# Talking-heads attention with a squared-ReLU FFN: turning q and k straight from their loaded layout, scores a block earlier, deeper gathers

## Chip, cores, metric

The kernel runs on 1 core of one Trainium2 chip. The metric is device microseconds of one execution, as a median of runs. Engines: PE (matmul; PEld are its weight loads), DVE (vector), ACT (scalar), GpSimd (POOL in the profile), SP (issues DMAs). The few timed executions of the kernel before that were slow (one on chip 0, two on chip 7) are left out of the ratios.

## The reference

```python
# q, k, v: (8, 12, 448, 64); w_pre, w_post: (12, 12)
scores = np.matmul(q, k.transpose(0, 1, 3, 2)) / sqrt(64)
scores = np.einsum('bhij,hg->bgij', scores, w_pre)       # mix the heads
attn   = softmax(scores, axis=-1)
attn   = np.einsum('bhij,hg->bgij', attn, w_post)        # mix again
x      = np.matmul(attn, v)                              # -> (3584, 768)
h      = np.maximum(x @ w_in, 0)                         # w_in (768, 2048)
out    = (h * h) @ w_out                                 # w_out (2048, 768)
```

## The kernel before

Each batch of 448 query rows is cut into blocks of 120, 120, 120 and 88 rows, and each block into tiles of 10 rows by 12 heads, so that mixing the heads is one matmul. A *step* handles two tiles; a batch has 23 steps. The FFN of a batch is filler for PE during the next batch. In the code, `at_step(i, f)` runs `f` at step i, and `hurry(units, w)` queues units of work for PE that become due w filler slots later (four slots per step). Names in the profile: `raw` is q or k as loaded, `rows` the same in another order, `s_ps` and `sq` scores, `sx` a gathered tile, `m_ps` the first mixing, `e` its exp, `d` the normalised tile, `at_ps` and `at` the second mixing, `ot_ps` and `xt` the product with v, `h_ps`, `hr`, `h` and `o_ps` the FFN.

```python
    def to_rows(raw, key, eng, parts=1):          # L87: a reordering copy
        t = work.tile([PR, NR, H, D], BF16, name="rows", tag="rows", bufs=2)
        w = H // parts
        for y in range(parts):
            eng.tensor_copy(out=t[:, :, w*y:w*y+w, :].rearrange("p r h d -> p h r d"),
                            in_=raw[:, w*y:w*y+w, :, :])
        rows[key] = t
    # ... start: to_rows(kraw, ..., nc.vector, 2); to_rows(qraw, ..., nc.vector, 2) ...

    def turn_unit(key, c):                        # 8 transposes of 128 columns
        src = rows[key]
        # ...
        for y in range(2):
            for r in range(NR):
                p = 2 * c + y
                nc.tensor.transpose(ps[:, S*y + PR*r : S*y + PR*r + PR],
                    src[:, r, 2*p:2*p+2, :].rearrange("p h d -> p (h d)"), ident[0:PR, 0:PR])
        nc.vector.tensor_copy(out=dst[...], in_=ps[...])          # kt or qt

    def scores(b, t, c):                          # a third of a block's scores
        for p in (2 * c, 2 * c + 1):
            ps = pair_bank("s_ps")                # one of 3 PSUM pairs
            # ... two matmuls ...
            nc.scalar.copy(out=sq[:, 2*p:2*p+2, :], in_=ps[:, :, 0:S])

    def pre(s):                                   # m_ps matmuls into a PSUM pair, exp on ACT, then
            nc.vector.tensor_scalar(out=d[0:TR, 0:S], in0=e[0:TR, :], ...)        # L304
    def post(s, y):                               # at_ps matmuls into a PSUM pair, then
            nc.vector.tensor_copy(out=ats[...], in_=ps[...])      # L325 frees the pair

    # plan: k of the next batch is copied at step 6, q at step 12
    at_step(i0 + 6 + 6*n, lambda key=key: to_rows(raws.pop(key), key, nc.gpsimd))
    at_step(i0 + 6 + 6*n, lambda key=key: hurry(turn_units(key), 6))
    # main loop, per step: pre; fill; scores of the NEXT block at its steps 0, 1, 3;
    #   gathers up to AHEAD = 6 tiles; filler; post of two steps ago
```

The softmax here doesn't subtract the row's maximum and nothing guards it: scores larger than these inputs give would overflow.

## Time and profile before

| kernel before | value | where |
|---|---|---|
| time | 755.97 us, median of 2 (755.44 to 756.49) | timed runs |
| span of the profiled execution (it took 748.7 us, about 7 less than the timed ones) | 746.8 us | page |
| PE, DVE, ACT, GpSimd busy | 83, 66, 61, 30% | page |
| PE and PEld both idle, up to PE's last instruction | 120.8 us | worked out: their records laid together |
| batches 1 to 6 | 85.1 us each | worked out: from first `e` to first `e` |

The page of the kernel before: busy us, then the span in 40 slices, in tenths (PEclk is the granted clock).

```profile
span 746.8 us, 15596 instructions
PE 620.1 (83%) x5898; PEld 368.1 (49%) x5898; DVE 491.2 (66%) x868; ACT 451.9 (61%) x1097; POOL 226.6 (30%) x250
PE   3375679779978898889988898799989797899897
PEclk9986768999989999999999999999999999999999
...
L87 POOL COPY rows<-raw 112x3072 bf16<-112x3072 bf16 x14 | 40.7, 2904 | 22.3 <-DMA raw<-in_q_dram 15.9
L304 DVE TENSOR_SCALAR d_109<-e,rc 120x448 bf16<-120x448 f32 x60 | 48.7, 812 | 1.1
```

PE is the busiest engine. The clock dips in the first quarter, where PE has little work. The last two lines give busy us and mean ns of one. The mean of `d_109` is 812 ns while most instances take about 450 ns, so a few must be very long.

PE's waits between 60 and 650 us in the list of waits (us in total, times, longest):

```profile
PE s_ps L273 <- DVE at_120 L325: 17.2, 9, 3.9
PE m_ps L294 <- DMA sx<-sq: 15.8, 15, 3.6
PE s_ps L273 <- DVE at_119 L325: 8.4, 6, 2.8
PE s_ps L273 <- DVE at_118 L325: 8.2, 7, 2.3
...
```

Scores wait 34 us here for a PSUM pair that DVE's eviction of `at_ps` frees, and the first mixing waits 16 us for a gathered tile. Why DVE is late stands in the timeline around 216 us (start, us, engine, line, out<-in, count). First GpSimd:

```profile
216.02 2.74 POOL L87 COPY rows<-raw 112x3072 bf16<-112x3072 bf16 x1
218.72 0.93 POOL L218 TENSOR_TENSOR h_2795<-hr 128x448 bf16<-128x448 f32 x1
```

Then DVE in the same stretch:

```profile
216.35 3.55 DVE L304 TENSOR_SCALAR d_106<-e,rc 120x448 bf16<-120x448 f32 x1
219.82 1.13 DVE L304 TENSOR_SCALAR d_107<-e,rc 120x448 bf16<-120x448 f32 x1
220.87 1.15 DVE L325 CAST at_120<-at_ps 112x960 bf16<-112x960 f32 x1
```

And PE:

```profile
219.36 0.36 PE L273 MATMUL s_ps<-kt_71,qt_69 64*128 64x448 bf16 x2
222.07 0.37 PE L273 MATMUL s_ps<-kt_71,qt_69 64*128 64x448 bf16 x2 [2.35 <-DVE at_120 L325]
```

Read the three together. `d_106` starts just after the GpSimd copy has started and ends at 219.9, after the copy and the GpSimd instruction behind it. It took 3.55 us in place of 0.45. Of DVE's frequent instructions only those into `d` are stretched like this: the six evictions of `at_ps` that start during one of the copies of this run take 1.14 to 1.16 us, as elsewhere. The eviction behind it in DVE's order ends at 222.0, and the second half of the scores stands waiting for that pair for 2.35 us.

Whole view of the `d` line: the windows view for that line alone (stretch, its length, DVE busy with count, clock, DMA share, GB/s; the stretch is longer than any span, so it holds all).

```profile
0.00:820.00 820.00, 206.75 (x360) 0.95 0.51 90
```

360 instructions of 0.45 us, whose records overlap at their ends by some 15 us in all, would be about 148 us.

### The profile page before, as it was taken

To read this page: it belongs to the slowest core of one execution; us is meant where nothing else is said; L and a number is where in the kernel's file an instruction comes from. 1 tells how busy PE (TensorE), PEld (TensorE's weight loads), DVE (VectorE), ACT (ScalarE), POOL (GpSimd) and SP (SyncE) were. 2 spreads that over 40 slices of the span, in tenths; PEclk is the share of its full clock that TensorE was granted. 3 is DMA by queue.
4 is the path that set the end of the run, shared out by engine and by line. 5 is a ranking of instruction groups with operands and counts; after the bars stand their busy time and mean duration, and the time that the engine had idled before them with its cause. 6 is when DMAs were issued, how large, how long until landed. Compare 5 with 4: busy or idle time off the path is not lost. (4 is left out here: it accounts for less than half of the span.)

```text
span 746.8 us, 15596 instructions
## 1 busy us (share of the span) xinstructions
PE 620.1 (83%) x5898; PEld 368.1 (49%) x5898; DVE 491.2 (66%) x868; ACT 451.9 (61%) x1097; POOL 226.6 (30%) x250
## 2 busy tenths in 40 slices
PE   3375679779978898889988898799989797899897
PEld 2043445445545554455555554455545564455554
DVE  2166768786678766886678766787677766566400
ACT  2363577557666566676676566576676576685241
POOL 5351004561044400462044400562034400340070
PEclk9986768999989999999999999999999999999999
DMA  9869534885455565657446464637456455333202
GB/s 125 133 115 213 105 74 86 150 141 112 95 100 83 70 127 108 97 83 125 88 98 98 71 128 100 107 64 112 110 102 96 61 100 105 74 70 64 64 5 71
DMA packets 94735, 73.38 MB, mean 98 GB/s; under 512 B 7108, under 2 KB 94660, under 8 KB 94660
## 3 DMA queue, kind: packets, MB, share of 16 engines
q1 hardware_dynamic: 55682, 49.57, 32.0%
q0 software_dynamic: 38848, 22.81, 23.2%
q8 instruction: 46, 0.75, 0.4%
q14 instruction: 29, 0.24, 0.1%
q10 hardware_dynamic: 130, 0.01, 0.0%
HBM read 45.63 MB, written 11.01 MB: 76 GB/s over the span
## 5 line engine op out<-in xcount | busy, mean ns | idle before, releaser
L297 ACT ACTIVATE e<-m_ps 120x448 f32<-120x448 f32 x360 | 193.0, 544 | 134.5 <-issue 61.8
L275 ACT CAST sq<-s_ps 128x896 bf16<-128x896 f32 x192 | 166.6, 915 | 24.4 <-PE s_ps L273 24.4
L294 PE MATMUL m_ps<-sx,pre_w 120*128 120x448 bf16 x360 | 112.6, 385 | 37.1 <-DMA sx<-sq 32.5
L300 DVE RECIPROCAL rc<-sm 120x2 f32<-120x2 f32 (+1 forms) x184 | 29.9, 162 | 144.1 <-ACT e L297 143.8
L217 ACT ACTIVATE hr<-h_ps 128x448 f32<-128x448 f32 x128 | 70.3, 550 | 73.5 <-PE h_ps L213 56.6
L325 DVE CAST at_119<-at_ps 112x960 bf16<-112x960 f32 (+1 forms) x63 | 71.0, 1128 | 12.2 <-PE at_ps L320 11.5
L325 DVE CAST at_118<-at_ps 112x960 bf16<-112x960 f32 (+1 forms) x63 | 71.0, 1128 | 10.3 <-PE at_ps L320 9.7
L297 ACT ACTIVATION_READ_ACCUMULATOR e<-m_ps 120x1 f32 x360 | 73.5, 204 | 0.0
L325 DVE CAST at_120<-at_ps 112x960 bf16<-112x960 f32 (+1 forms) x58 | 65.8, 1135 | 7.3 <-PE at_ps L320 6.7
L248 ACT COPY osb<-o_ps 128x384 f32<-128x384 f32 x56 | 26.9, 480 | 56.2 <-PE o_ps L243 54.7
L273 PE MATMUL s_ps<-kt_71,qt_69 64*128 64x448 bf16 x192 | 34.4, 406 | 22.6 <-DVE at_120 L325 7.0
L273 PE MATMUL s_ps<-kt_72,qt_70 64*128 64x448 bf16 x192 | 32.2, 375 | 23.5 <-DVE at_120 L325 10.2
L294 PEld LDWEIGHTS <-pre_w 120*128 120x128 bf16 x360 | 32.5, 105 | 37.1 <-DMA sx<-sq 17.0
L304 DVE TENSOR_SCALAR d_109<-e,rc 120x448 bf16<-120x448 f32 x60 | 48.7, 812 | 1.1
L87 POOL COPY rows<-raw 112x3072 bf16<-112x3072 bf16 x14 | 40.7, 2904 | 22.3 <-DMA raw<-in_q_dram 15.9
L304 DVE TENSOR_SCALAR d_106<-e,rc 120x448 bf16<-120x448 f32 x60 | 46.2, 770 | 0.9
L213 PE MATMUL h_ps<-xt,w_0_126 128*128 128x448 bf16 x192 | 42.8, 363 | 0.1
L213 PE MATMUL h_ps<-xt,w_3_129 128*128 128x448 bf16 x192 | 41.2, 353 | 1.0 <-DVE xt L206 0.9
L165 PE MATMUL t_ps<-ident,rows 112*128 112x112 bf16 x384 | 35.4, 254 | 7.6 <-DVE rows L87 7.6
L213 PE MATMUL h_ps<-xt,w_1_127 128*128 128x448 bf16 x192 | 41.2, 353 | 0.2
L213 PE MATMUL h_ps<-xt,w_2_128 128*128 128x448 bf16 x192 | 41.1, 352 | 0.0
L206 DVE TENSOR_TENSOR xt<-ot_ps,bvec 128x360 bf16<-128x360 f32 (+1 forms) x64 | 31.7, 505 | 10.7 <-PE ot_ps L199 9.6
(475 smaller groups left out, 1200.9 us busy)
## 6 DMA issues: line engine op xcount, KB each, us to landing
sx<-sq SPq DMA_DIRECT2D x352, 105.0 KB
raw<-in_k_dram POOLq DMA_DIRECT2D x21, 224.0 KB, 7.6
raw<-in_q_dram POOLq DMA_DIRECT2D x21, 224.0 KB, 6.9
v_67<-in_v_dram POOLq DMA_DIRECT2D x12, 224.0 KB, 6.3
v_68<-in_v_dram POOLq DMA_DIRECT2D x12, 224.0 KB, 6.7
out_dram<-osb SPq DMA_DIRECT2D x16, 168.0 KB
out_dram<-osb SPq DMA_DIRECT2D x16, 144.0 KB
out_dram<-osb SPq DMA_DIRECT2D x16, 120.0 KB
```

The source lines that it names most:

```text
L87: eng.tensor_copy(out=t[:, :, w * y:w * y + w, :].rearrange("p r h d -> p h r d"), in_=raw[:, w * y:w * y + w, :, :])
L165: nc.tensor.transpose(ps[:, S * y + PR * r:S * y + PR * r + PR], src[:, r, 2 * p:2 * p + 2, :].rearrange("p h d -> p (h d)"), ident[0:PR, ...
L206: nc.vector.tensor_tensor(out=xts[b][:, cs, BQ * t:BQ * t + n], in0=pv[:, :, 0:n], in1=bvecs[b][:, cs].unsqueeze(2).to_broadcast([P, 3, n] ...
L213: nc.tensor.matmul(ps[:, 0:S], lhsT=w1[ft // 4][:, c2, 128 * (ft % 4):128 * (ft % 4) + 128], rhs=xts[b][:, c2, :], start=(c2 == 0), stop=( ...
L217: nc.scalar.activation(out=hr[:, :], in_=ps[:, 0:S], func=ACT.Relu)
L273: nc.tensor.matmul(ps[:, hh, 0:S], lhsT=qt[x][r, p, BQ * t:BQ * t + 128], rhs=kt[x][r, p, :], start=True, stop=True)
L275: nc.scalar.copy(out=sq[:, 2 * p:2 * p + 2, :], in_=ps[:, :, 0:S])
L294: nc.tensor.matmul(ps[:, y, 0:S], lhsT=pre_w[0:rows, :], rhs=sx[0:rows, :], start=True, stop=True)
L297: nc.scalar.activation(out=e[0:TR, :], in_=ps[0:TR, y, 0:S], func=ACT.Exp, scale=SCALE, accum_out=sm[0:TR, y:y + 1])
L300: nc.vector.reciprocal(out=rc[0:TR, 0:len(ms)], in_=sm[0:TR, 0:len(ms)])
L304: nc.vector.tensor_scalar(out=d[0:TR, 0:S], in0=e[0:TR, :], scalar1=rc[0:TR, y:y + 1], scalar2=1.0 / S, op0=ALU.mult, op1=ALU.subtract)
L325: nc.vector.tensor_copy(out=ats[(b, t)][0:PR, :, :, i0:i0 + TQ * n].rearrange("p r g (y i) -> p y (r g) i", i=TQ), in_=ps[0:PR, 0:n, 0:NR ...
```

## The change

Intent: (A) drop the reordering copies and transpose each head from the loaded layout, into the lower or upper 64 partitions, and give `raw` a second buffer; the transposes also become due one filler slot after their step, in place of six; (B) issue a block's scores about a block earlier; (C) gather up to ten tiles ahead in place of six; also a third `hr` buffer.

```diff
-    rows = {}
-    def to_rows(raw, key, eng, parts=1): ...
-    kraw, qraw = new_raw(), vt[1]
+    kraw, qraw = new_raw(), new_raw()          # raw: bufs 1 -> 2
-    to_rows(kraw, ("k", 0), nc.vector, 2)
-    to_rows(qraw, ("q", 0), nc.vector, 2)
...
-                p = 2 * c + y
-                nc.tensor.transpose(ps[:, S * y + PR * r:S * y + PR * r + PR],
-                                    src[:, r, 2 * p:2 * p + 2, :].rearrange("p h d -> p (h d)"), ident[0:PR, 0:PR])
+                for hh in range(2):
+                    nc.tensor.transpose(ps[64 * hh:64 * hh + 64, S * y + PR * r:S * y + PR * r + PR],
+                                        src[:, 4 * c + 2 * y + hh, r, :], ident[0:PR, 0:PR])
...                                             # hr: bufs 2 -> 3, sx: bufs 7 -> 12
-    AHEAD = 6
+    AHEAD = 10
-                at_step(i0 + 6 + 6 * n, lambda key=key: to_rows(raws.pop(key), key, nc.gpsimd))
-                at_step(i0 + 6 + 6 * n, lambda key=key: hurry(turn_units(key), 6))
+                at_step(i0 + 6 + 6 * n, lambda key=key: hurry(turn_units(key), 1))
+    for n in range(1, len(blocks)):            # first[x]: first step of block x
+        for c in range(3):
+            bursts.setdefault(first[blocks[n - 1]] - 1 + c, []).append((n, c))
...                                             # main loop
-                at_steps = (0, 1, 2) if t == 3 else (0, 1, 3)
-                if nb < len(blocks) and j in at_steps:
-                    scores(*blocks[nb], at_steps.index(j))
...
+                for n, c in bursts.get(i, []):
+                    scores(*blocks[n], c)
...
```

More of the change, by code (lines that the diff above doesn't have):

```diff
@@ L73, in new_raw @@
     def new_raw():
-        return work.tile([PR, H, NR, D], BF16, name="raw", tag="raw", bufs=1)
+        return work.tile([PR, H, NR, D], BF16, name="raw", tag="raw", bufs=2)
     def load_heads(t, src, b, h0, n):
@@ L78, in load_heads @@
                             in_=src[b, h0:h0 + n].rearrange("h (p r) d -> p h r d", r=NR))
-    rows = {}
-    def to_rows(raw, key, eng, parts=1):
-        t = work.tile([PR, NR, H, D], BF16, name="rows", tag="rows", bufs=2)
-        w = H // parts
-        for y in range(parts):
-            eng.tensor_copy(out=t[:, :, w * y:w * y + w, :].rearrange("p r h d -> p h r d"),
-                            in_=raw[:, w * y:w * y + w, :, :])
-        rows[key] = t
-    kraw, qraw = new_raw(), vt[1]
+    kraw, qraw = new_raw(), new_raw()
+    raws = {("k", 0): kraw, ("q", 0): qraw}
     for h0 in (0, 6):
@@ L157, in turn_unit @@
     def turn_unit(key, c):
-        src = rows[key]
+        src = raws[key]
         dst = (kt if key[0] == "k" else qt)[key[1] % 2]
@@ L215, in ffn1_unit @@
         h2 = work.tile([P, S], BF16, name="h2", tag="h2", bufs=FT + 1)
-        hr = work.tile([P, S], F32, name="hr", tag="hr", bufs=2)
+        hr = work.tile([P, S], F32, name="hr", tag="hr", bufs=3)
         nc.scalar.activation(out=hr[:, :], in_=ps[:, 0:S], func=ACT.Relu)
@@ L279, in gather @@
         n = min(TQ, BLOCKS[t] - TQ * m)
-        sx = work.tile([P, S], BF16, name="sx", tag="sx", bufs=7)
+        sx = work.tile([P, S], BF16, name="sx", tag="sx", bufs=12)
         nc.sync.dma_start(out=sx[0:H * n, :], in_=sqs[(b, t)][TQ * m:TQ * m + n, :, :])
@@ L367 @@
     until = [0]
-    raws = {}
     def start_raw(key):
@@ L388 @@
                         raws[key], src, b + 1, 4 * y, 4))
-                at_step(i0 + 6 + 6 * n, lambda key=key: to_rows(raws.pop(key), key, nc.gpsimd))
-                at_step(i0 + 6 + 6 * n, lambda key=key: hurry(turn_units(key), 6))
+                at_step(i0 + 6 + 6 * n, lambda key=key: hurry(turn_units(key), 1))
             for y in range(3):
                 at_step(i0 + 13 + y, lambda y=y, b=b: load_heads(vt[(b + 1) % 2], v, b + 1, 4 * y, 4))
+    first = {}
+    for i, (b, t, ms) in enumerate(steps):
+        first.setdefault((b, t), i)
+    bursts = {}
+    for n in range(1, len(blocks)):
+        for c in range(3):
+            bursts.setdefault(first[blocks[n - 1]] - 1 + c, []).append((n, c))
     def gathers(limit):
@@ L410 @@
         gathers(AHEAD)
+        for n, c in bursts.get(-1, []):
+            scores(*blocks[n], c)
         for i in range(len(steps) + LAG):
@@ L426 @@
                 fill(share)
-                nb = blocks.index((b, t)) + 1
-                at_steps = (0, 1, 2) if t == 3 else (0, 1, 3)
-                if nb < len(blocks) and j in at_steps:
-                    scores(*blocks[nb], at_steps.index(j))
-                    if j == at_steps[2]:
-                        done_scores.add(blocks[nb])
+                for n, c in bursts.get(i, []):
+                    scores(*blocks[n], c)
+                    if c == 2:
+                        done_scores.add(blocks[n])
                 gathers(AHEAD)
```

## The prediction

> **What bounds the kernel now.** The page has PE busy 83% of the 746.8 us span, DVE 66%, ACT 61%. Laying matmuls and weight loads together, PE stands still about 121 us: 31 in the first 60 us, 15 from 60 to 110, 64 from 110 to 600, 11 after. This idle time is what can be won.  The list of waits says what ends PE's idle time there: scores wait for a PSUM pair that DVE's eviction of at_ps frees (about 32 us), weighted sums wait for the same eviction (11), pre-mixing waits for gathered tiles by DMA (6), ACT the rest.
>
> **Why DVE is late.** The 14 GpSimd copies raw to rows (2.75 us median) hold DVE up. In the timeline, DVE's TENSOR_SCALAR into d beside such a copy takes 1.7 to 5.2 us where its median is 0.45 (about 3 us lost at each of the 12 copies after 100 us). The Trainium skill, "SBUF — State Buffer", section "SBUF: two separate sides", says the port pair shared by GpSimd and DVE is an exclusive lock for a whole instruction; these records agree. PE idles about 2.7 us in each copy's span plus the next 7 us: 32 us over the twelve, of which some 12 would be idle anyway.
>
> **What the change does.**
> 1. Removes those copies: estimate 20 to 25 us off the path.
> 2. Start: no DVE copies (0.56 us each) ahead of the first evictions. These stand in DVE's order behind the last rows copy and the weight setup, so the first score matmul comes at 13.9 us though its q and k halves had landed by 8 us. The third group of scores ends at 21.3 us; I expect 17 to 18.5: 3 us.
> 3. Transposes double, 384 to 768, each to 64 partitions. The ot_ps matmuls, also in 64-partition halves, take 1.45 us for 48, about 27 ns each, so neighbouring halves overlap (the skill's "TensorEngine Tiling (Array Packing)", "Key Properties": tiles operate independently). 16 halves should take 0.45 to 0.55 us against 0.57 for 8 whole transposes. Cost 0 to 5 us.
> 4. Scores one block ahead, ten tiles ahead: PE's waits for sx (9 us from 60 to 110, 7 later, 13 in the first 60) mostly go: 8 to 12 us, chiefly in the first batch.
> 5. Unchanged: three PSUM pairs, the number of score bursts (96), the eviction per step, the last 50 us of pure FFN. So s_ps waits do not vanish; clustering three transpose units around a burst in one step gives some idle back. Loads, no longer paced by GpSimd's waits, crowd the DMA engines (86% busy in the first 60 us) under the first gathers.
>
> Sum: minus 22, 3 and 10, plus 3 for transposes and 0 to 5 given back: minus 30 to 38.
>
> **Predicted: 720 us**, 8 in 10 between 704 and 739. Faster by over 2%: 0.87; within 2%: 0.11; slower: 0.02.
>
> **What would show it.** No d longer than 1.3 us in steady state; DVE busy down by 35 to 45 us; PE idle from 110 to 600 scaled down to about 40; sx waits after 60 us under 5 us in total; t_ps groups of 16 halves within 0.65 us; first exp before 26 us; PE busy sum almost unchanged.
>
> **What would make it wrong.** Halved transposes that do not overlap (adds 20 us); early loads that starve the first gathers; the steady state held by the ACT-DVE-PSUM loop rather than by the stalls, so that DVE's freed time turns into other waits (gain under 15 us); or, the other way, the earlier bursts also removing s_ps waits (gain over 50).

## The result

The kernel after takes 697.98 us (median of 2, 696.18 to 699.78), ratio 0.9233 (95% interval 0.9127 to 0.9339). The prediction was 720 us, with a range of 704 to 739: the direction was right and the gain too small. A ratio here is the mean time of one kernel's fast runs over that of the kernel before's fast runs of the same rounds, so it is not quite the ratio of the quoted medians.

The page of the kernel after:

```profile
span 694.3 us, 16351 instructions
PE 603.4 (87%) x6282; PEld 356.8 (51%) x6282; DVE 451.6 (65%) x864; ACT 451.7 (65%) x1097; POOL 184.2 (27%) x236
PE   4477789899889998899798997899889996999997
PEclk9999789999999999999999999999999999999999
...
L152 PE MATMUL t_ps<-ident,raw 112*64 112x112 bf16 x768 | 31.6, 234 | 7.0 <-DMA raw<-in_k_dram 6.2
L291 DVE TENSOR_SCALAR d_101<-e,rc 120x448 bf16<-120x448 f32 x60 | 33.4, 556 | 0.8
```

PE's waits between 60 and 650 us, from the top of the list:

```profile
PE s_ps L260 <- ACT e L284: 12.8, 18, 1.0
PE at_ps L307 <- ACT e L284: 11.6, 14, 2.6
...
PE s_ps L260 <- DVE at_115 L312: 2.7, 4, 0.8
...
```

The waits of scores for DVE shrank from 34 to 8 us. The wait for gathered tiles fell from 15.8 to 0.4 us in this stretch. What remains is mostly ACT. PE and PEld are both idle for 85.1 us in place of 120.8. And PE's own busy time fell by 17 us although its work did not shrink: the granted clock rose from 0.942 to 0.982.

The same place in a batch in the timeline of the kernel after, DVE:

```profile
190.82 0.61 DVE L291 TENSOR_SCALAR d_101<-e,rc 120x448 bf16<-120x448 f32 x1
191.36 0.43 DVE L291 TENSOR_SCALAR d_102<-e,rc 120x448 bf16<-120x448 f32 x1
...
192.78 1.14 DVE L312 CAST at_115<-at_ps 112x960 bf16<-112x960 f32 x1
```

and PE, where a group of 16 half transposes takes 0.58 us; 8 whole ones took 0.57 before:

```profile
188.93 0.58 PE L152 MATMUL t_ps<-ident,raw 112*64 112x112 bf16 x16
189.45 0.55 PE L260 MATMUL s_ps<-kt_71,qt_69 64*128 64x448 bf16 x4
...
193.52 0.36 PE L260 MATMUL s_ps<-kt_71,qt_69 64*128 64x448 bf16 x2 [0.91 <-ACT e L284]
```

The `d` line over the whole execution, in the windows view of the kernel after:

```profile
0.00:820.00 820.00, 168.89 (x360) 0.98 0.49 90
```

It is 37.9 us shorter than before.

### The profile page after: what moved, and what is told of

Its sections match the earlier page's. It is cut to its first block, busy times and chain, and to the rows that moved or that the text cites. A ratio compares the mean times of both kernels' runs of the same rounds, so it can differ in the third digit from the quotient of the medians.

```text
span 694.3 us, 16351 instructions
## 1 busy us (share of the span) xinstructions
PE 603.4 (87%) x6282; PEld 356.8 (51%) x6282; DVE 451.6 (65%) x864; ACT 451.7 (65%) x1097; POOL 184.2 (27%) x236
## 5 line engine op out<-in xcount | busy, mean ns | idle before, releaser
L281 PE MATMUL m_ps<-sx,pre_w 120*128 120x448 bf16 x360 | 104.7, 368 | 23.4 <-DMA sx<-sq 10.8
L287 DVE RECIPROCAL rc<-sm 120x2 f32<-120x2 f32 (+1 forms) x184 | 29.8, 162 | 106.4 <-ACT e L284 106.2
L312 DVE CAST at_115<-at_ps 112x960 bf16<-112x960 f32 (+1 forms) x58 | 65.6, 1134 | 14.3 <-PE at_ps L307 14.0
L260 PE MATMUL s_ps<-kt_71,qt_69 64*128 64x448 bf16 x192 | 33.6, 393 | 15.3 <-ACT e L284 8.5
L260 PE MATMUL s_ps<-kt_72,qt_70 64*128 64x448 bf16 x192 | 31.4, 364 | 11.9 <-ACT e L284 6.4
L152 PE MATMUL t_ps<-ident,raw 112*64 112x112 bf16 x768 | 31.6, 234 | 7.0 <-DMA raw<-in_k_dram 6.2
L152 PEld LDWEIGHTS <-raw 112*64 112x64 bf16 x768 | 24.2, 122 | 21.2 <-issue 12.0
L291 DVE TENSOR_SCALAR d_101<-e,rc 120x448 bf16<-120x448 f32 x60 | 33.4, 556 | 0.8
L291 DVE TENSOR_SCALAR d_104<-e,rc 120x448 bf16<-120x448 f32 x60 | 31.5, 525 | 1.0
```

What stands on the lines that cost most here:

```text
L152: nc.tensor.transpose(ps[64 * hh:64 * hh + 64, S * y + PR * r:S * y + PR * r + PR], src[:, 4 * c + 2 * y + hh, r, :], ident[0:PR, 0:PR])
L260: nc.tensor.matmul(ps[:, hh, 0:S], lhsT=qt[x][r, p, BQ * t:BQ * t + 128], rhs=kt[x][r, p, :], start=True, stop=True)
L281: nc.tensor.matmul(ps[:, y, 0:S], lhsT=pre_w[0:rows, :], rhs=sx[0:rows, :], start=True, stop=True)
L287: nc.vector.reciprocal(out=rc[0:TR, 0:len(ms)], in_=sm[0:TR, 0:len(ms)])
L291: nc.vector.tensor_scalar(out=d[0:TR, 0:S], in0=e[0:TR, :], scalar1=rc[0:TR, y:y + 1], scalar2=1.0 / S, op0=ALU.mult, op1=ALU.subtract)
L312: nc.vector.tensor_copy(out=ats[(b, t)][0:PR, :, :, i0:i0 + TQ * n].rearrange("p r g (y i) -> p y (r g) i", i=TQ), in_=ps[0:PR, 0:n, 0:NR ...
```

## The experiments

The question was why 58 us and not 36. Two views stood against each other: theory A, that the GpSimd copies holding DVE up were the main cost; theory B, that the earlier scores and deeper gathers carried the gain. Later the question became what about the copies costs: the hold of one long instruction on DVE, GpSimd's occupied time, the copy as work, or the lowered PE clock.

The diffs below are abridged: some of their lines are words that stand for code. This table gathers all runs. "d" is DVE busy on the `d` line from the windows view where I give it. Batch times are worked out from the profiled execution, from first `e` to first `e` ("start" is the first `e` of all). The medians belong to their own chip, so compare by ratio. The last four columns come from one profiled execution each, which can lie some us off the median: that of before took 748.7 us, that of bursts_only 754.7 (the slowest of its four), that of before_split 733.2 (the slowest of its four) and that of bursts_split 719.5 (the fastest of its four). Differences of a few us between these columns are within that.

| run | median us | ratio (95% interval) | start | batch 0 | batches 1-6, mean | d |
|---|---|---|---|---|---|---|
| before | 756.0 | 1 | 28.6 | 80.5 | 85.1 | 206.8 |
| after | 698.0 | 0.923 (0.913-0.934) | 27.5 | 66.6 | 79.4 | 168.9 |
| direct_only (A alone) | 713.6 | 0.950 (0.944-0.956) | 28.8 | 78.5 | 80.6 | 171.7 |
| bursts_only (B alone) | 750.9 | 0.998 (0.995-1.002) | 29.6 | 72.5 | 87.6 | 214.0 |
| copies_back | 727.2 | 0.966 (0.959-0.972) | 28.6 | 67.5 | 84.3 | 198.7 |
| rows_on_dve | 807.6 | 1.074 (1.071-1.077) | 34.4 | 78.9 | 94.3 | |
| after_near (A and B) | 699.9 | 0.927 (0.921-0.934) | 28.8 | 66.4 | 79.6 | 169.3 |
| after_late (A and C) | 723.4 | 0.957 (0.951-0.964) | 27.9 | 77.0 | 80.6 | 171.7 |
| before_warm | 756.2 | 1.002 (0.995-1.009) | 29.1 | 86.8 | 85.4 | |
| after_warm | 694.1 | 0.921 (0.915-0.927) | 28.3 | 63.6 | 79.6 | |
| bursts_shifted | 746.4 | 0.989 (0.985-0.993) | 28.7 | 73.4 | 86.2 | 196.8 |
| copies_warm | 726.7 | 0.963 (0.958-0.968) | 28.5 | 67.7 | 84.4 | 198.1 |
| after_gate | 692.4 | 0.917 (0.914-0.921) | 24.4 | 68.1 | 79.2 | |
| gate_warm | 692.1 | 0.919 (0.913-0.925) | 24.2 | 65.6 | 79.6 | |
| copies_split | 697.1 | 0.926 (0.920-0.931) | 27.6 | 64.5 | 80.0 | 174.2 |
| after_again | 698.1 | 0.924 (0.920-0.928) | 28.5 | 66.6 | 79.4 | |
| gate_again | 693.8 | 0.919 (0.915-0.923) | 24.0 | 68.7 | 79.4 | |
| after_hr2 | 696.1 | 0.923 (0.918-0.929) | 28.2 | 67.1 | 79.0 | |
| before_split | 728.9 | 0.967 (0.960-0.975) | 33.8 | 76.6 | 82.6 | 179.0 |
| bursts_split | 723.7 | 0.962 (0.954-0.970) | 33.2 | 66.7 | 82.4 | 179.2 |

### direct_only: part A alone

```diff
 # after, but
-    AHEAD = 10                  # sx bufs 12
+    AHEAD = 6                   # sx bufs 7
-    scores from bursts
+    scores of the next block at its steps 0, 1, 3, as before
```

> The change without its second half: q and k turned straight from the loaded layout, no copies to rows, raw twice, but scores at the old steps and six tiles ahead. Theory A (the GpSimd copies that hold DVE up, with the half clock that follows PE's idle time, carry most of the gain of 58 us): 705 to 722 us, ratio to the kernel before 0.935 to 0.955, no d over 2 us. Theory B (scores a block ahead and more gathered tiles carry most, by taking the wait for a PSUM pair and for sx away): 735 us or more, ratio 0.97 or higher.

Measured: ratio 0.950, about 38 us. Theory A holds: two thirds of the gain are here. The `d` line in its windows view:

```profile
0.00:820.00 820.00, 171.74 (x360) 0.96 0.50 90
```

That is 35 us less than before, nearly the gain itself. The scores' wait for DVE, 34 us before (60 to 650 us), is 10.7 us here, so it is part A and not the earlier scores that takes this wait away.

### bursts_only: part B alone

```diff
 # before, but
-    scores of the next block at its steps 0, 1, 3
+    scores from bursts, one block ahead     # copies, AHEAD = 6 as before
```

> The kernel before with the scores one block ahead, all else as it was (rows copies on GpSimd, six tiles ahead: twelve sx buffers beside the rows tiles do not fit in SBUF). Theory A: 740 to 756 us, ratio 0.98 to 1.0, d still up to 3.5 us or more in each batch, s_ps waits for DVE still over 20 us. Theory B: 725 us or less, ratio 0.96 or lower, s_ps waits for DVE under 12 us.

Measured: no gain (0.998). Batch 0 became 8 us shorter and each later batch 2.5 us longer in the profiled executions. (By their spans this run was 6 us slower than before, by the timed ones 1 us faster; see the note above the table.) Its `d` line:

```profile
0.00:820.00 820.00, 214.02 (x360) 0.93 0.52 89
```

DVE is held 7 us longer than before; six of the long `d` instructions of this run take 4.45 to 4.6 us (one in the kernel before), and scores wait for DVE still more (45 us of PE's idle time from 60 to 650 us, against 34). Part B with twelve `sx` buffers beside the `rows` tiles does not fit into SBUF (the kernel before with twelve is refused when it is built: 88.4 KB per partition for the pool, 84.8 left), so B and C without A could not be tried.

### copies_back: the copies alone put back into the kernel after

```diff
+    def idle_copy(key):         # into the v tile that the next load overwrites
+        spare = vt[key[1] % 2][:, :, :, :].rearrange("p h r d -> p (h r d)")
+        nc.gpsimd.tensor_copy(out=spare.rearrange("p (r h d) -> p h r d", r=NR, h=H), in_=raws[key][:, :, :, :])
...
+                at_step(i0 + 6 + 6 * n, lambda key=key: idle_copy(key))
```

> The kernel after with the 14 GpSimd copies put back at their steps, into the v tile that the next load overwrites; nothing reads what they write, the result stays right. Theory A: 28 to 40 us slower than the kernel after, ratio to before 0.96 to 0.975, one d of 1.7 to 5 us beside nearly every copy, and more half-clock time. Theory B: under 10 us slower, ratio 0.925 to 0.935.

Measured: ratio 0.966, so 29 us by the medians and, by the ratios of this run and after_again, (0.9657 - 0.9239) x 754 = 32 us slower than the kernel after. Nothing reads what these copies write. One of them, with DVE beside it:

```profile
366.20 2.74 POOL L79 COPY v<-raw 112x3072 bf16<-112x3072 bf16 x1
366.68 2.88 DVE L296 TENSOR_SCALAR d<-e,rc 120x448 bf16<-120x448 f32 x2
```

The `d` line of the whole run:

```profile
0.00:820.00 820.00, 198.72 (x360) 0.96 0.50 90
```

It grew by 29.8 us over the kernel after, again the size of the loss. PE's idle time grew by only 15 us, and its busy time (PE and PEld laid together) by 16 at unchanged PE work, with the granted clock at 0.958. The hold reaches PE by other waits than in the kernel before (60 to 650 us, copies_back against after): scores wait for DVE's eviction hardly more (9.3 against 8.0 us), but ACT's exp waits 15 us in place of 8 for a `d` instruction, scores wait 20 us in place of 13 for that exp, and `h_ps` waits 8 us for evictions of `kt` and `qt` that stand behind the `d`. So the wait that heads the list is not the only path by which a late DVE costs time. This is the point at which the prediction had looked at the wrong number.

### rows_on_dve: the copies moved to DVE (a miss)

```diff
-to_rows(raws.pop(key), key, nc.gpsimd)
+to_rows(raws.pop(key), key, nc.vector, 2)
```

> The kernel before with the 14 later copies moved from GpSimd to DVE, two halves of 0.56 us each. Theory A (what costs is the long hold of GpSimd on DVE, not the copy's work): DVE loses about 36 us of stalls and gains 16 us of copies, 720 to 740 us, ratio 0.955 to 0.98, no d over 2 us. If the copy as such is what costs, wherever it runs: 750 us or more, ratio 0.99 or higher.

Measured: 7% slower. By the number this falls under the second expectation (750 us or more), but the list of waits shows why the run says little about the copies: DVE now stood before each copy until its load had landed.

```profile
DVE rows L87 <- DMA raw<-in_k_dram: 45.9, 15, 5.8
DVE rows L87 <- DMA raw<-in_q_dram: 28.9, 14, 5.2
```

The hold itself was gone, as the first expectation had it (no `d` over 1.7 us, 164.0 us on the `d` line). The experiment traded it for a new wait on DMA, so it did not answer its question. copies_split and before_split, below, do.

### after_near and after_late: which half of the second part

```diff
 # after_near: after, but AHEAD = 6 and 7 sx buffers; scores stay one block ahead
 # after_late: after, but scores at the old steps; gathers stay ten ahead
```

> The kernel after with gathers only six tiles ahead (seven sx buffers); scores stay one block ahead. Theory P (early scores and deep gathers need each other: without depth the early scores are not fetched early, without early scores there is nothing to fetch): 707 to 714 us, ratio to before 0.943 to 0.953, as direct_only, sx waits of PE 25 us or more. Theory Q (early scores alone bring the second part of the gain): 696 to 702 us, ratio 0.923 to 0.935.

> The kernel after with the scores at the steps of the kernel before; gathers stay ten tiles ahead. Theory P: 707 to 714 us, ratio 0.943 to 0.953, sx waits 25 us or more. Theory R (depth of gathers alone brings the second part): 696 to 702 us, ratio 0.923 to 0.935, sx waits under 14 us.

Measured: after_near 0.927, within the interval of the kernel after; after_late 0.957, no better than direct_only. Theory Q holds: early scores alone bring the second part, (0.950 - 0.927) x 751 = 17 us, or 23 us by the ratios of after_late and after_near, which ran on one chip; gathering deeper brings nothing measurable. Most of it lies in batch 0 (78.5 against 66.4 us) and 1 us in each of the six later batches (80.6 against 79.6). PE's wait for `sx` is 32 us in direct_only and 17 in after_near. A gather can start only when the scores of its block are in SBUF.

### before_warm, after_warm, copies_warm: is the lower clock a cost of its own?

Four matmuls of 448 columns, into a PSUM bank that nobody reads: in each of the first 26 steps (before_warm, after_warm), or in the middle of the score bursts at the copies' steps and the next ones (copies_warm, on copies_back).

```diff
+    def warm(n):
+        ps = bank("w_ps")
+        for _ in range(n):
+            nc.tensor.matmul(ps[:, 0:S], lhsT=ident[:, :], rhs=kt[0][:, 0, :], start=True, stop=True)
```

> The kernel before with four extra matmuls of 448 columns, whose result nobody reads, in each of the first 26 steps (about 0.75 us of PE at full clock, 19 us in all). Theory C (the half clock of the first 130 us costs time of its own, some 10 to 17 us): steps 3 to 35 run at full clock and the whole is no slower: 738 to 752 us, ratio 0.98 to 1.0, batch 0 at least 4 us shorter. If the half clock only fills time in which PE would wait anyway: 755 to 770 us, ratio 1.005 to 1.025, batch 0 not shorter.

> The same extra matmuls in the kernel after. Theory C: batch 0 (66.6 us in the profile) shortens by 2 to 6 us, total 692 to 697 us, no cold m_ps after 45 us. Otherwise: 700 to 710 us.

> copies_back with four extra matmuls of 448 columns, read by nobody, in the middle of the score bursts of the copies' steps, where PE waits for DVE. Theory C (the half clock that follows the wait costs time of its own, about half of what a copy costs): fewer cold m_ps than the 16 after batch 0 in copies_back, 712 to 722 us, ratio 0.947 to 0.96. If the clock is only a symptom: 725 to 745 us, ratio 0.963 or higher.

Measured: before_warm gained nothing (1.002). I count an `m_ps` matmul over 450 ns as cold, as most take 350 and the others about 560. In batch 0 of before_warm these fell from 31 of 45 to 14 of 45, so the clock expectation was met only in part, and the batch grew. copies_warm brought the cold ones after batch 0 from 16 down to 6 and the granted clock from 0.958 to 0.975, and stayed at 0.963 against 0.966. after_warm landed in the range of theory C (694 us, and batch 0 at 63.6 against 66.6 us, with 4 cold ones of 45 in place of 24), but its 0.921 lies within the interval of the kernel after, and gate_warm below gained nothing over after_gate. So in the copies' stretches the lower clock looks mainly like a companion of the wait. These matmuls also cost PE time (26 steps or 28 bursts of about 0.75 us each, some 20 us in all) and yet none of these runs became clearly slower, so a gain of the clock of its own, hidden under that cost, is not excluded.

### bursts_shifted: copies moved away from the bursts

```diff
 # bursts_only, but
-  q loads from step 7;  copies at steps 6 and 12
+  q loads from step 9;  copies at steps 8 and 14
```

> bursts_only with the GpSimd copies, and the loads of q, two steps later, so that each copy falls behind the three score bursts (steps 5, 6, 7 and 11, 12, 13 of a batch) and not among them. Theory I (early scores gained nothing alone because their bursts fell on the copies' steps, where DVE is held and frees no PSUM pair): batches 1 to 6 fall from 87.6 us to 83 to 85.5, batch 0 stays at 71 to 74, total 728 to 742 us, ratio 0.967 to 0.985. Theory J (early scores are no gain in this kernel for another reason): 747 us or more, ratio 0.995 or higher.

Measured: 0.989, between both expectations. The stretch of steps 5 to 9 fell from 18.4 to 14.3 us, but steps 15 to 23 grew from 25.9 to 30.3. So moving the copies away from the bursts won only part of what was hoped. What made the later steps longer, the copies at their new place or the transposes that now come later, no run separates.

### copies_split: the same copies in six pieces

```diff
 # copies_back, but
-        nc.gpsimd.tensor_copy(out=spare..., in_=raws[key][:, :, :, :])
+        for y in range(6):
+            nc.gpsimd.tensor_copy(out=spare...[:, 2*y:2*y+2, :, :], in_=raws[key][:, 2*y:2*y+2, :, :])
```

> copies_back with each GpSimd copy cut into six pieces of two heads, same bytes, same steps. Theory D (the cost of a copy is the time for which one GpSimd instruction holds a DVE instruction up, passed on nearly one to one): if DVE gets in between pieces, the time by which d is stretched in sum falls from 51 us to 28 to 40, no d over 1.8 us from a copy, total 702 to 716 us, ratio 0.93 to 0.952. If DVE does not get in between pieces, or if the time that GpSimd is occupied is what costs: d stretched by 48 us or more or total 722 us or more, ratio 0.96 or higher.

Measured: 0.926, the same as the kernel after (0.924 on the same chip). The loss is gone although GpSimd is occupied for longer than with one copy. The timeline around 373 us, GpSimd:

```profile
372.86 3.71 POOL L80 COPY v<-raw 112x512 bf16<-112x512 bf16 x6
```

and DVE in the same stretch:

```profile
373.19 1.24 DVE L298 TENSOR_SCALAR d<-e,rc 120x448 bf16<-120x448 f32 x2
374.36 1.14 DVE L161 COPY qt<-t_ps 128x896 bf16<-128x896 bf16 x2
375.42 1.14 DVE L319 CAST at<-at_ps 112x960 bf16<-112x960 f32 x1
```

Two `d` instructions passed in 1.24 us in the midst of the six pieces. In copies_back two took 2.88 us at this place, and up to 3.55 beside other copies. The `d` line of the whole run:

```profile
0.00:820.00 820.00, 174.15 (x360) 0.98 0.49 90
```

So neither the copy's bytes nor GpSimd's occupied time is what costs. The length of a single hold is. The loss vanished more fully than I had expected (702 to 716 us).

### before_split and bursts_split: the same cut in the kernel before

```diff
-to_rows(raws.pop(key), key, nc.gpsimd)
+to_rows(raws.pop(key), key, nc.gpsimd, 6)     # bursts_split: with the early scores too
```

> The kernel before with each of its 14 GpSimd copies cut into six pieces; nothing else is touched, rows, transposes and scores stay as they were. Theory D (the long single hold is what cost, not the copy): the stretch of d falls from 60 us to 24 to 32, 708 to 722 us, ratio 0.943 to 0.957, as direct_only. If turning straight from the loaded layout brought a gain of its own: 730 us or more, ratio 0.967 or higher.

> The same with the scores one block ahead. Theory D, with early scores that are worth something only once the long holds are gone: 697 to 708 us, ratio 0.924 to 0.94, batch 0 at 66 to 74 us. If early scores need the direct transposes: 712 us or more, ratio 0.945 or higher.

Measured: before_split 0.967, about 25 us from a change of one argument, with `d` at

```profile
0.00:820.00 820.00, 178.99 (x360) 0.97 0.51 90
```

28 us less than before. It lies outside the range that I had given theory D (0.943 to 0.957), and by its ratio in that of the other one: the long hold is most of what part A wins, but not all. The rest of part A (direct transposes, due sooner, with a second `raw` buffer: no run separates these three) brings another 1.7% (0.967 against 0.950, on different chips, and the intervals nearly touch). 5 us of that is the start, which is later in before_split (33.8 against 28.8 us) and in bursts_split too (33.2), so it is hardly chance. In before_split GpSimd issues the loads of q from 23.0 us, ahead of the first gather at 23.05, and not from 24.6 as before; the second gathered tile then keeps PE waiting 5.3 us in place of 0.9. That is the crowding that after_gate shows below, though no run tests it here. `d` is also still held 7 us longer than in direct_only.

bursts_split gains 5 us more by the medians of the same chip (723.7 against 728.9), not clear of noise by its interval: in the profile batch 0 is 10 us shorter and the later batches are the same. So of their 17 to 23 us beside direct transposes early scores bring about 5 here, and none beside whole copies. I can argue a reason (in the order of PE's instructions the transposes from `rows` still stand just ahead of the product with v, where the direct ones come a little over one step sooner; from 60 to 650 us PE waits 27 us before `ot_ps` in this run, 21 in before_split and 5 in the kernel after), but no run isolates it.

### after_gate, gate_warm, after_again, gate_again: the start

The first scores came earlier in the kernel after, but the first `e` hardly did (27.5 against 28.6 us). The first gathers are issued at 18.6 us and the first mixing starts at 25.8; by then GpSimd has issued loads of the next batch:

```profile
18.60 17.75 SPq L268 DMA_DIRECT2D sx<-sq  x16
25.79 0.56 PE L281 MATMUL m_ps<-sx,pre_w 120*128 120x448 bf16 x1 [7.41 <-DMA sx<-sq]
```

The gate holds these loads until the fourth gathered tile is there:

```diff
+    at_step(1, lambda: nc.gpsimd.tensor_copy(out=seen[0:1, 0:1], in_=landed[3][0:1, 0:1]))
```

> The kernel after with GpSimd held, by a one-element copy, until the fourth gathered tile has landed, before it issues the loads of the next batch. Theory G (the start did not get shorter because these loads crowd the first gathers): first exp at 22 to 25 us in place of 27.5, total 692 to 697 us, ratio 0.916 to 0.924. If the first gathers are slow by themselves: first exp after 26 us and no gain, ratio 0.925 or higher.

> after_gate with the extra matmuls of after_warm in the first 26 steps: the candidate for a better kernel. If both help and add up: 686 to 692 us, ratio 0.908 to 0.918. If they do not add: as after_warm, 692 to 697 us, ratio 0.917 to 0.925.

> The kernel after, unchanged, timed on the same chip as the others of this call. All theories: ratio to before 0.92 to 0.93, 694 to 702 us, time by which d is stretched 20 to 25 us.

> after_gate once more, beside the kernel after on the same chip. If its gain is real: 3 to 6 us faster than the kernel after, ratio to before 0.913 to 0.92, first exp 22 to 25 us. If it was the chip: within 2 us of the kernel after.

The timeline of after_gate at the start:

```profile
18.81 8.55 SPq L271 DMA_DIRECT2D sx<-sq  x9
22.59 0.56 PE L285 MATMUL m_ps<-sx,pre_w 120*128 120x448 bf16 x1 [4.00 <-DMA sx<-sq]
25.63 0.18 POOL L368 COPY seen<-sx 1x1 bf16<-1x1 bf16 x1 [18.89 <-DMA sx<-sq]
26.18 0.71 POOL L77 DMA_DIRECT2D raw<-in_k_dram  x1 [0.38 <-PE m_ps L285]
```

Issue to use of the first tile fell from 7.2 us to 3.8, so theory G holds: the loads crowded the gathers. Side by side on one chip, five rounds each: 693.8 us with the gate and 698.1 without (0.919 and 0.924; the intervals overlap a little, but after_gate had shown the same, at 692.4 us). Part of the 4 us won at the start is given back in batch 0. This is the fastest version I ran, by about 0.6%. The extra matmuls (gate_warm, 692.1 us) add nothing clear of noise to it.

### after_hr2: the third hr buffer

```diff
-hr = work.tile([P, S], F32, name="hr", tag="hr", bufs=3)
+hr = work.tile([P, S], F32, name="hr", tag="hr", bufs=2)
```

> The kernel after with two hr buffers, as before. If the third hr buffer has no part in the gain: within 3 us of the kernel after, ratio 0.92 to 0.932. If it has: 5 us or more slower, ratio 0.933 or higher.

Measured: 0.923, as the kernel after. It has no part in the gain.

## Why the prediction missed

Right, with the direction:

- The copies held DVE, and with them gone DVE's busy time fell by 39.6 us (35 to 45 predicted). Two `d` instructions over 1.3 us remain (1.5 and 1.8), so "no d longer than 1.3 us" was nearly right.
- Doubling the transposes is close to free: 0.58 us for 16 halves against 0.57 for 8, as the overlap of half-width matmuls on `ot_ps` had suggested. The allowance of 3 us for it was not needed; the 0 to 5 us "given back" no run measured by itself.
- PE's waits for gathered tiles nearly ended: in the list from 60 to 650 us they are 0.4 us in place of 15.8. PE's idle time fell by 36 us, in line with the sum of 30 to 38. That it met the sum is partly luck: by copies_back the copies' own share of the idle time was 15 us and not 20 to 25.

Wrong:

- **The step that failed is the first term: "Removes those copies: estimate 20 to 25 us off the path".** It was derived from PE's idle time in and just after the copies, less an ordinary share. Putting the copies back cost 29 to 32 us, and cutting them in the kernel before saved about 25, with the rest of A making it 38. (The 25 alone would fit the term, but in that run `d` is still held and the start is 5 us late.) In each of these three the change in time is close to the change of DVE's time on the `d` line (29.8, 27.8 and 35.0 us). That is no law: bursts_shifted has 17 us less on that line than bursts_only and is 7 us faster, and rows_on_dve has the least of all and is the slowest. The prediction had a nearer number in its own text ("about 3 us lost at each of the 12 copies"), and discounted it by PE's idle time.
- **"PE busy sum almost unchanged" failed with it, and is why pricing by idle time fell short.** The busy sum fell by 17 us. After waits of PE the trace has stretches of half clock (in the kernel before, after the wait of 2.34 us that ends at 308.1, the windows view gives a granted clock of 0.50 from 309.3 to 312.5), in which matmuls take longer and count as busy. copies_back shows it with the same PE work: of the loss, 15 us are idle time and 16 busy time. Worked out from the clock records, PE was busy at half clock for 57 us there and for 22 in the kernel after; half of the difference, 17 us, is the extra busy time. The share of idle time is no constant: by the profiled spans it is 15 of 31 us here, 27 of 33 from before to direct_only, and 1 of 16 from before to before_split. That the lower clock is a cost of its own is not supported: copies_warm and before_warm raised it and gained nothing; for the start it stays open.
- **"So s_ps waits do not vanish" failed too:** the scores' waits for DVE fell from 34 to 8 us. The prediction had named a way to a gain over 50 us, "the earlier bursts also removing s_ps waits", and the gain was 58, but it did not come that way: part A alone brings these waits to 11 us, early scores alone raise them to 45.
- **The fourth term, "8 to 12 us", measured 17** (direct_only to after_near; 23 from after_late), with the same split: PE's idle time differs by 9 us between the first two and its busy time by 10. And it belongs to the early scores alone; the deeper gathers had no part.
- **The second term, the start, measured 1 us or less and not 3** (27.5 and, in after_again, 28.5 against 28.6). The third group of scores did end by 17 us as predicted, and then the gathers took 7.2 us, since the loads, no longer paced, stood in their way. The prediction named this risk and gave it no number. after_gate shows that it was worth about 4 us.

The changes do not add up singly: A alone 38, B alone 1, both 55 us (after_near). What stays open is why early scores pay in full only beside direct transposes, and what of part A, beyond the long holds, brings its last 13 us.

## What to carry to other kernels

In this kernel a GpSimd copy beside DVE work cost by how long one instruction was, not by how much was copied: look for DVE instructions with a mean far above their median, and cut the GpSimd instruction next to them into pieces before designing it away. When you price a stall, take the time lost on the engine that is held, if its work feeds a loop that PE waits for; PE's idle time alone showed about half of it in copies_back, since PE's busy time grew too. Treat that as a first estimate and confirm it by putting the stall back alone, as copies_back does. When an ordering or a copy that paced your loads goes away, ask what the loads will collide with.

## What the Trainium skill lacked or had wrong

- "SBUF — State Buffer", section "SBUF: two separate sides", says that GpSimd and DVE share a port pair as an exclusive lock held for a whole instruction. The runs agree, and add two things that it lacks. First, the remedy: the same 14 copies in six pieces each cost nothing (697 us) where whole ones cost 29 us (727). Secondly, DVE can stay held past the instruction that it met: beside a copy of 2.74 us the `d` instruction took 3.55, until the next GpSimd instruction had ended as well, and up to 5.20 in the same run with two of them behind the copy; yet between the six pieces it mostly got through (in before_split one `d` was still held for 2.92 us).
- "TensorE: Matmul & The Clock Gate", in its table "Why this matters for your kernels", advises to keep PE free of gaps so that the clock stays up. In this kernel raising the granted clock from 0.958 to 0.975 by extra matmuls (copies_warm, some 20 us of PE time) changed nothing measurable in the time (0.966 and 0.963); the page doesn't say how to tell a lowered clock that costs from one that only accompanies a wait.
- "TensorEngine Tiling (Array Packing)", section "Performance Considerations", recommends column tiling for a stationary side of 64 or fewer but gives no number for transposes: here 16 transposes to 64 partitions took 0.58 us, 8 to 128 partitions 0.57.
